# Attention in steps of two units, routing-table products behind their marks

## The chip, the core and the metric

One NeuronCore of a Trainium2 chip runs the whole program. The metric is the device time in microseconds (us) of one execution. The kernel before took 796.1 us, the median of three runs (795.92 to 799.77). Of the core's engines this kernel uses TensorE (PE, with its weight loads PEld), VectorE (DVE), ScalarE (ACT), GpSimd (POOL) and the DMA queues of SyncE (SP) and GpSimd.

## The reference

An attention with a global and a local window, followed by a mixture of experts with the two best of eight.

```
scores = q @ k.T / sqrt(64) - slope[h] * dist          # 4 x 8 heads, 768 positions, head size 64
keep   = (key < n_global) | (0 <= row - key < n_local)  # 8 global, 96 local
a      = softmax(where(keep, scores, -1e9));  x = a @ v  # -> 3072 tokens x 512
noisy  = x @ w_gate + log1p(exp(x @ w_noise)) * noise   # 3072 x 8
top2 weights = softmax over the two largest of noisy
out[token] += weight * relu(x[token] @ w1[e]) @ w2[e]   # for the token's two experts, 512 -> 1024 -> 512
```

## The kernel before, in words

Every engine's instructions run in the order in which the program writes them; semaphores hold an instruction until its inputs are there. Nothing reorders them, so an instruction that waits holds all behind it on its engine.

**Attention.** The 3072 rows are 24 groups of 128, and a group has four units of two heads: 96 units. `score(n)` makes the scores of units n and n+1 on TensorE (L609); VectorE adds the bias and takes the minimum of the negated scores (L616), ScalarE takes exponentials (L620). `trans(n)` transposes a unit's exponentials with four 128x128 products (L632), and ScalarE copies them back (L634). `attend(n)` multiplies them with the values in tiles of 64 columns (L654); after every second unit VectorE divides by the sums (L660 to L663). The loop takes one unit per step: `trans(n)`, at even n `score(n + 2)`, `attend(n - 2)`, then what `todo` lists for this step. `tick()` is called between these and four times inside `score`; each call lets the active routings go one step on (routings 0 and 1 at every second call).

**Gate.** A finished group goes through `gate_t` (transposes, L285), `gate_l` (products with the gate's weights, L293, copied by ScalarE at L296) and `gate_s` (L299), at m, m + 2 and m + 3, where m is the step after the group's last `attend`.

**Routing.** Five runs of groups (`SEG`) are routed one after the other by the generator `route(r)`. It computes noise and the two best experts on VectorE, positions by products with triangles and ones (L375 to L379), and then for each of its 2 x w slots a *mark* (128x128 one-hot, GpSimd, L408) and an *entry* (128x64, VectorE, L409); products of marks and entries (L415) sum up the table of row numbers, which `find` turns into the lists that gathers use. Routing 2 gives the rows of the first four tiles of expert 0. GpSimd also splits the weights of expert 0 into two halves of precision (`split`, L205 and L206), between marks. `scales` takes the largest weight of each piece by VectorE's reductions (L149).

**Experts.** `up(e, c, f)` makes one of eight groups of hidden units (12 products), for c = 0 (512 tokens) and c = 1 (300 tokens); `down` and `down_t` come back to 512. Ahead of each of the eight first groups of expert 0, `steps_of` says how many steps the two unfinished routings, 3 and 4, are taken on: `[10, 60]` and `[0, 25, 4, 14, 1, 100]`. Then the second tiles of expert 0 and the first of expert 1 are gathered by GpSimd's indirect DMAs, four `down` follow, and the gathered tiles are turned by TensorE. At the end of attention the first four tiles are scaled (`ready`, `rest`) and turned (`turn_pe`, L264 to L267) the same way.

Of the kernel before, what the change touches and what calls it, by code (L numbers as in the profile page):

```python
# [35 lines left out]
def tile_local_global_attention_then_moe(  # L36
# [46 lines left out]
    def bank16(tag, bufs):  # L83
        return psum.tile([P, 1024], F16, name=tag, tag=tag, bufs=bufs)
# [174 lines left out]
    def turn_pe(e, t, ps=None):  # L259
        x = xp.pop((e, t))  # L260
        m = height(t)
        ps = (spare_bank(bank16) if ps is None else ps)[:, :2 * KC * m].rearrange("p (k t) -> p k t", k=2 * KC)
        for k in range(2 * KC):
            nc.tensor.transpose(ps[:, k], x[:m, k * P:(k + 1) * P], ident16[:m, :m])  # L264
        y = place(t, m)
        nc.scalar.activation(y[:, :KC], ps[:, :KC], AF.Copy)  # L266
        nc.vector.tensor_copy(y[:, KC:], ps[:, KC:])  # L267
# [36 lines left out]
    def route(r):  # L304
# [99 lines left out]
        for i in range(w):  # L404
            for j in range(2):
                x = gp.tile([P, P], F16, name="mark", bufs=2 * SW)
                y = gp.tile([P, E * (TT + 1)], F16, name="entry", bufs=2 * SW)
                nc.gpsimd.tensor_scalar(x, row, slf[:, 0, i, j:j + 1], None, op0=OP.is_equal)  # L408
                nc.vector.tensor_scalar(y, col, slf[:, 1, i, j:j + 1], val[:, a + i:a + i + 1],  # L409
                                        op0=OP.is_equal, op1=OP.mult)  # L410
                marks.append((x, y))
                yield
        ps = lg[:, (NT * 2 + SW + 1) * E:(NT * 2 + SW + 1 + TT + 1) * E]
        for i, (x, y) in enumerate(marks):
            nc.tensor.matmul(ps, x, y, start=i == 0, stop=i + 1 == len(marks))  # L415
# [24 lines left out]
    with ExitStack() as actx:  # L440
# [182 lines left out]
        def trans(n):  # L623
            g, hp, b, i = geo(n)
            w = 2 * P if i else P
            ps = bank("at", 2)[:, :2 * w]
            p4 = ps.rearrange("p (x c t) -> p x c t", x=2, t=P)
            x = A.pop(n)
            for s in range(2):
                for c in range(w // P):  # L630
                    a = AW - P if c + 1 == w // P else 0
                    nc.tensor.transpose(p4[:, :, c, s * Q:(s + 1) * Q], x[:, s, a:a + P], ident)  # L632
            AT[n] = aw.tile([P, 512], F32, name="at", bufs=4)[:, :2 * w]
            nc.scalar.activation(AT[n], ps, AF.Copy)  # L634
# [3 lines left out]
        def attend(n):  # L638
            g, hp, b, i = geo(n)
            w = 2 * P if i else P  # L640
            x = AT.pop(n)
            if hp % 2 == 0:
                pav[g, hp // 2] = bank("av", 2)[:, :4 * D1].rearrange("p (h d) -> p h d", h=4)
            ps = pav[g, hp // 2]
            blocks = [(vs[g], P, w - P)]
            if i:
                blocks.insert(0, (vp[g], NP + NG, 0))
            for s in range(2):
                h = 2 * hp + s
                c = slice(h * D1, (h + 1) * D1)  # L650
                for t, kk, c0 in blocks:
                    for y in range(2):
                        a = s * w + c0 + y * Q
                        nc.tensor.matmul(ps[y * Q:(y + 1) * Q, h % 4], x[:kk, a:a + Q], t[:kk, c],  # L654
                                         start=kk < P or not i, stop=kk == P, tile_position=(0, y * Q))
            if hp % 2:
                if hp == 1:
                    XR[g] = gp.tile([P, H, D], F32, name="xr", bufs=2)
                den = aw.tile([P, 4], F32, name="den", bufs=2)
                nc.vector.tensor_scalar(den, ps[:, :, D], 1e-9, None, op0=OP.add)  # L660
                nc.vector.reciprocal(den, den)
                h0 = 2 * hp - 2
                nc.vector.tensor_mul(XR[g][:, h0:h0 + 4], ps[:, :, :D],  # L663
                                     den[:, :, None].to_broadcast([P, 4, D]))
# [3 lines left out]
        def at(n, f, *a):  # L668
            todo.setdefault(n, []).append((f, a))
# [70 lines left out]
        if not windowed:  # L740
            gate_consts()
            route_consts()
            empty_rows()
            for j in range(NZ):
                zero_out(j)
            for g in range(NT):
                whole(g)
            load_w(5)
            for x in 1, 2:
                for _ in scales(0, x):  # L750
                    pass
            for j in range(FC):
                split(0, 1, j)
            load_w()
            for t in range(TA):
                ready(0, t)
                rest(0, t)
                turn_pe(0, t)
        else:
            NPAIR = NT * HP  # L760
            LAG = 2
            for k in range(HP):
                at(k, biases, bias, dist, (2 * k, 2 * k + 1))
            at(4, gate_consts)
            at(10, route_consts)
            at(12, empty_rows)
            for g in range(NT):
                b, i = divmod(g, NB)
                n = g * HP
                if g + 3 < NT:  # L770
                    at(n + 2, load_v, g + 3)
                m = n + HP - 1 + LAG + 1
                if g + 1 < NT:
                    at(m, gate_t, g)
                    at(m + 2, gate_l, g)
                    at(m + 3, gate_s, g)
                if i % NBH == 0 and g + NBH < NT:
                    for k in range(NBH):
                        at(n + 4 * k, load_qk, *divmod(g // NBH + 1, 2), k)
                for r, (a, z) in enumerate(SEG):  # L780
                    if g == z - 1:
                        routes[m + 3] = route(r)
            for j in range(NZ):
                at(16 + 9 * j, zero_out, j)
            for j in 20, 26, 32, 46, 64, 76:
                at(j, load_w)
            for x, places in (1, (30, 32, 37, 39, 42, 45)), (2, (44, 46, 56, 58, 61, 64)):
                first = scales(0, x)
                for j in places:
                    at(j, next, first)  # L790
            for j in range(FC):
                at(48 + 2 * j, split, 0, 1, j, nc.gpsimd)
            for t in range(TA):
                at(NPAIR - 5 + t, ready, 0, t)
                at(NPAIR - 4 + min(t, 2), rest, 0, t)

            score(0)
            for n in range(NPAIR + LAG):
                if n < NPAIR:
                    trans(n)  # L800
                if n % 2 == 0 and n + 2 < NPAIR:
                    score(n + 2)
                tick()
                if n == NPAIR - 1:
                    for x, _ in [y for y in active if y[1] <= CLOSE]:
                        for _ in x:
                            pass
                if n >= NPAIR - 1:
                    t = n - NPAIR + 1
                    turn_pe(0, t, bank16("sc", 3))  # L810
                    if t == 2:
                        turn_pe(0, 3, bank16("sc", 3))
                if LAG <= n:
                    attend(n - LAG)
                tick()
                for f, a in todo.pop(n, []):
                    f(*a)
                if n in routes:
                    active.append((routes.pop(n), [z for a, z in SEG].index((n - LAG - 4) // HP + 1)))
            assert len(routes) == 1  # L820
            pending = (pending + [x for x, _ in active] + list(routes.values()))[-2:]


    with ExitStack() as mctx:
# [71 lines left out]

        steps_of = [10, 60], [0, 25, 4, 14, 1, 100]

        for f in range(FC):
            for x, n in enumerate(steps_of):
                if f < len(n):
                    for _ in range(n[f]):
                        next(pending[x], 0)
            if NZ + f < (DUMP + N) // P // 2:
                zero_out(NZ + f)
            if f == 0:
                load_w()
            if f == 2:  # L910
                for h in range(2):
                    nc.scalar.activation(xpb[32:, h * Dm:(h + 1) * Dm], zero[32:MP], AF.Copy)
            up(0, 0, f, f < 3, {4: gate_t, 8: gate_l, 11: gate_s} if f == 0 and windowed else {})
            for j in range([0, 0, 0, 2, 3, 4, 6, 7][f], [0, 0, 2, 3, 4, 6, 7, 8][f]):
                split(0, 2, j)
        for t in range(TB):
            gather(0, TA + t)
        for t in range(2):
# [163 lines left out]
```

## Time and profile before

| | |
|---|---|
| median of the runs shown | 796.1 us |
| profiled execution | 794.64 us, its span 792.8 us |
| TensorE busy | 741.3 us, 93% of the span |
| VectorE, ScalarE, GpSimd busy | 487.8, 360.1, 212.5 us |
| mean granted TensorE clock | 0.981 |
| attention ends, expert 0 begins | 211.67 us |
| expert 0's first eight groups end | 251.86 us |

A busy time is the union of an engine's instruction times. The granted clock is the share of full speed that TensorE got. Waits are given with the engine that waited, the line it stood at and what released it.

### The profile page before, as it was taken

Reading aid. Unit: us, or ns where it says so; the run is one execution under the profiler, and the core shown is the slowest. Engines: PE = TensorE matmul, PEld = TensorE weight load, DVE = VectorE, ACT = ScalarE, POOL = GpSimd, SP = SyncE. Lnnn points to the kernel's source line nnn. Section 1 sums busy time; section 2 is a strip of 40 time slices with the busy share of each in tenths; the row PEclk is TensorE's granted clock in tenths of the full one; section 3 lists DMA queues with packets and bytes.
Section 4 is the critical chain, followed back from the end, with each engine's and each line's share of the span. In section 5 each row is a group of like instructions: output and inputs, shape, how many; then the busy total and the mean of one; then the engine's idle time right before and its main releaser. Section 6 shows DMA issues by size and latency. Waiting matters only on the chain.

```text
span 792.8 us, 16589 instructions
## 1 busy us (share of the span) xinstructions
PE 741.3 (93%) x6279; PEld 460.0 (58%) x6279; DVE 487.8 (62%) x1635; ACT 360.1 (45%) x744; POOL 212.5 (27%) x225
## 2 busy tenths in 40 slices
PE   6999969888849988999999999999999999999995
PEld 4777747666514465556465564656556465565662
DVE  6557877867665466676386476738737664872500
ACT  5777767666432343433345244333424434342411
POOL 2000085241233412221403213141331314122013
PEclk9999989999988999999999999999999999999999
DMA  7899766762602596468448755745964684472015
GB/s 214 283 284 303 207 202 200 227 208 67 222 20 58 87 214 135 135 131 176 99 133 144 124 173 100 165 99 147 142 130 155 104 162 97 109 101 32 1 16 74
DMA packets 107257, 112.58 MB, mean 142 GB/s; under 512 B 53184, under 2 KB 65680, under 8 KB 107168
## 3 DMA queue, kind: packets, MB, share of 16 engines
q1 hardware_dynamic: 95232, 84.51, 39.1%
q0 software_dynamic: 11936, 26.92, 19.5%
q8 instruction: 51, 0.84, 0.4%
q14 instruction: 38, 0.31, 0.1%
HBM read 71.61 MB, written 28.10 MB: 126 GB/s over the span
## 4 chain that ended last, share of the span: by engine, by line
PE 48%; issue 10%; POOL 2%; DVE 1%; DMA 0%; ACT 0%; POOLq 0%; ACTq 0%
PE av L873 14%; PE sc L840 12%; PE at L840 12%; PE av L883 8%; POOL out_dram L858 2%; PE lg L894 0%; PE sc L894 0%; DMA out_dram<-y,ids 0%; DVE wmx L149 0%; PE sc L160 0%; ACT w1h L203 0%; DVE xp L249 0%; PE sc L153 0%; DVE l L238 0%; POOL xg L222 0%
## 5 line engine op out<-in xcount | busy, mean ns | idle before, releaser
L858 POOL DMA_INDIRECT out_dram<-y,ids x56 | 88.7, 1584 | 238.4 <-ACT y L857 234.8
L840 PEld LDWEIGHTS <-w1h 128*128 128x128 f16 x1024 | 100.1, 99 | 70.2 <-issue 4.0
L840 PE MATMUL at<-xx,w1h 128*128 128x300 f16 (+1 forms) x512 | 129.7, 342 | 0.9 <-ACT xx L266 0.8
L840 PE MATMUL sc<-xx,w1h 128*128 128x300 f16 (+1 forms) x512 | 126.2, 335 | 0.0
L222 POOL DMA_INDIRECT xg<-xd,ids x56 | 58.1, 1038 | 169.9 <-DVE hl L851 103.7
L873 PE MATMUL av<-w2h,hh 128*128 128x512 f16 x256 | 97.1, 379 | 0.0
L873 PE MATMUL av<-w2l,hh 128*128 128x512 f16 x256 | 97.0, 379 | 0.0
L873 PE MATMUL av<-w2h,hl 128*128 128x512 f16 x256 | 97.0, 379 | 0.0
L840 PE MATMUL at<-xx,w1l 128*128 128x512 f16 (+1 forms) x256 | 87.1, 340 | 0.0
L620 ACT ACTIVATE a<-ns,mx 128x168 f32<-128x168 f32 (+1 forms) x192 | 70.1, 421 | 35.7 <-DVE mx L616 28.0
L840 PE MATMUL sc<-xx,w1l 128*128 128x512 f16 (+1 forms) x256 | 85.8, 335 | 0.0
L873 PEld LDWEIGHTS <-hh 128*128 128x128 f16 x512 | 49.5, 98 | 56.3
L851 DVE SCALAR_TENSOR_TENSOR hl<-sc,hh 128x300 f16<-128x300 f32 (+1 forms) x63 | 36.4, 577 | 69.3 <-ACT hh L850 69.3
L850 ACT ACTIVATE hh<-at 128x300 f16<-128x300 f32 (+1 forms) x62 | 31.1, 502 | 100.4 <-PE at L840 100.4
L149 DVE TENSOR_REDUCE wmx<-raw 128x1 f32<-128x1024 f32 x64 | 76.4, 1207 | 0.0
L883 PE MATMUL av<-hl,w2h 128*128 128x300 f16 x256 | 74.1, 290 | 2.0 <-DVE hl L851 2.0
L883 PE MATMUL av<-hh,w2h 128*128 128x300 f16 x256 | 74.6, 291 | 0.6 <-DVE yt L886 0.3
L883 PE MATMUL av<-hh,w2l 128*128 128x300 f16 x256 | 74.3, 290 | 0.0
L840 PEld LDWEIGHTS <-w1l 128*128 128x128 f16 x512 | 50.6, 99 | 39.0 <-issue 2.4
L851 DVE SCALAR_TENSOR_TENSOR hl<-at,hh 128x300 f16<-128x300 f32 (+1 forms) x62 | 35.6, 574 | 60.9 <-ACT hh L850 60.9
L616 DVE CUSTOM_DVE_ANT_0 ns<-sc,bias 128x168 f32<-128x168 f32 (+1 forms) x192 | 54.3, 319 | 23.0 <-PE sc L609 18.0
L242 ACT ACTIVATE xp<-xg,up 128x512 f16<-128x512 f32 x48 | 34.5, 719 | 74.1 <-DVE up L240 61.4
(173 smaller groups left out, 1234.6 us busy)
## 6 DMA issues: line engine op xcount, KB each, us to landing
raw<-in_w SPq DMA_DIRECT2D x32, 1024.0 KB
out_dram<-zero SPq DMA_DIRECT2D x14, 512.0 KB
vs<-in_v SPq DMA_DIRECT2D x24, 260.0 KB
qs<-in_q SPq DMA_DIRECT2D x24, 256.0 KB
xd<-xr SPq DMA_DIRECT2D x24, 256.0 KB
ks<-in_k SPq DMA_DIRECT2D x20, 272.0 KB
vp<-in_v SPq DMA_DIRECT2D x20, 195.0 KB
ks<-in_k SPq DMA_DIRECT2D x4, 464.0 KB
```

Of the source, the lines that this page charges most:

```text
L149: nc.vector.tensor_reduce(m[:, i:i + 1], t[:, i % 2 * n:(i % 2 + 1) * n], op=OP.max, axis=AX.X, apply_absolute_value=True)
L222: nc.gpsimd.indirect_dma_start(out=xg[e, t], out_offset=None, in_=xd[:n], in_offset=bass.IndirectOffsetOnAxis(ap=rows(e, t), axis=0), boun ...
L242: nc.scalar.activation(y[:m, :Dm], x[:, :Dm], AF.Copy, scale=u)
L616: nc.vector.tensor_tensor_reduce(out=ns[:, s, :w], in0=ps[:, s], in1=bias[:, hp, s] if i else bias0[:, hp, s], scale=-scale, scalar=3e38, ...
L620: nc.scalar.activation(A[m][:, s, c:c + w], ns[:, s, :w], AF.Exp, bias=mx[:, s:s + 1], scale=-1.0)
L840: nc.tensor.matmul(ps, w[e % 2][:, k, fs], xx[c][:, x + k, :hh[c].shape[2]], start=n == 0, stop=n == 3 * KC - 1)
L850: nc.scalar.activation(hh[c][:, f], ps, AF.Relu)
L851: nc.vector.scalar_tensor_tensor(hl[c][:, f], ps, 0.0, hh[c][:, f], op0=OP.max, op1=OP.subtract)
L858: ins = nc.gpsimd.indirect_dma_start(out=out, out_offset=bass.IndirectOffsetOnAxis(ap=rows(e, t), axis=0), in_=y, in_offset=None, bounds_c ...
L873: nc.tensor.matmul(ps, x[0][:, f, cols], w[e % 2][:, f], start=n == 0, stop=n == 3 * FC - 1)
L883: nc.tensor.matmul(ps, w[e % 2][:, f, cols], x[1][:, f], start=n == 0, stop=n == 3 * FC - 1)
```

## The change

The attention loop takes two units per step: both `trans`, then `score`, then both `attend`, then the todo lists of both. The products of a table come 8 steps of the routing (2 for the later ones) behind its last mark, and every second mark is made by VectorE. `gate_s` moves to m + 4, the routing's start with it. Weight loads, scales, splits and zero fills get other steps. Routing 4's products of positions and its marks move to the sixth group of expert 0, its table behind the eighth.

```diff
-                nc.gpsimd.tensor_scalar(x, row, slf[:, 0, i, j:j + 1], None, op0=OP.is_equal)
+                (nc.vector if j else nc.gpsimd).tensor_scalar(x, row, slf[:, 0, i, j:j + 1], None, op0=OP.is_equal)
...
+        for _ in range(8 if r < CLOSE else 2 if r + 1 < len(SEG) else 0):
+            yield
         ps = lg[:, (NT * 2 + SW + 1) * E:(NT * 2 + SW + 1 + TT + 1) * E]
...
-                    at(m + 3, gate_s, g)
+                    at(min(m + 4, NPAIR + LAG - 1), gate_s, g)
...
-                        routes[m + 3] = route(r)
+                        routes[m + 4] = route(r)
             for j in range(NZ):
-                at(16 + 9 * j, zero_out, j)
-            for j in 20, 26, 32, 46, 64, 76:
+                at(56 + 4 * j, zero_out, j)
+            for j in 22, 32, 50, 58, 76, 86:
                 at(j, load_w)
-            for x, places in (1, (30, 32, 37, 39, 42, 45)), (2, (44, 46, 56, 58, 61, 64)):
+            for x, places in (1, (34, 36, 42, 44, 46, 48)), (2, (58, 60, 66, 68, 70, 72)):
...
-                at(48 + 2 * j, split, 0, 1, j, nc.gpsimd)
+                at(52 + 2 * j, split, 0, 1, j, nc.gpsimd)
...
-            for n in range(NPAIR + LAG):
+            for n in range(0, NPAIR + LAG, 2):
                 if n < NPAIR:
                     trans(n)
-                if n % 2 == 0 and n + 2 < NPAIR:
+                    trans(n + 1)
+                if n + 2 < NPAIR:
                     score(n + 2)
                 tick()
...
+                for u in range(2):
+                    if n == NPAIR:
+                        turn_pe(0, u, bank16("sc", 3))
+                    if n >= LAG:
+                        attend(n - LAG + u)
+                    tick()
+                if n == NPAIR:
+                    for t in range(2, TA):
+                        turn_pe(0, t, bank16("sc", 3))
+                for u in range(2):
+                    for f, a in todo.pop(n + u, []):
+                        f(*a)
                 tick()
...
-        steps_of = [10, 60], [0, 25, 4, 14, 1, 100]
+        steps_of = [10, 60], [0, 25, 0, 0, 0, 18]
...
+        for _ in pending[1]:
+            pass
         for t in range(TB):
             gather(0, TA + t)
```

## Rows read from the trace of the kernel before

**Rows 1.** The page: span and instructions.
```profile
span 792.8 us, 16589 instructions
```

**Rows 2.** Windows: stretch, length, busy PE, PEld, DVE, ACT, POOL (instructions), clock, DMA share, GB/s.
```profile
98.70:121.92 23.22, 16.48 (x231) 12.06 (x230) 15.64 (x76) 13.86 (x34) 19.68 (x22) 0.85 0.56 177
121.92:152.73 30.81, 29.41 (x522) 22.80 (x521) 26.50 (x159) 24.22 (x61) 16.10 (x18) 1.00 0.76 237
152.73:193.58 40.85, 36.19 (x571) 27.20 (x571) 28.18 (x191) 26.53 (x65) 10.94 (x15) 0.96 0.51 161
193.58:211.67 18.09, 13.00 (x204) 10.63 (x204) 16.17 (x72) 9.91 (x21) 5.49 (x9) 0.91 0.34 112
211.67:251.86 40.19, 28.07 (x133) 12.15 (x134) 19.38 (x78) 12.58 (x23) 12.97 (x15) 0.83 0.23 79
17.53:63.63 46.10, 45.54 (x777) 34.90 (x777) 26.09 (x158) 35.75 (x94) 1.73 (x8) 1.00 0.90 278
63.63:98.70 35.07, 33.54 (x596) 25.98 (x595) 29.68 (x167) 25.47 (x66) 1.09 (x1) 1.00 0.78 244
```

**Rows 3.** Waits of all engines: engine, line, releaser, total us, times, longest.
```profile
...
PE lg L299 <- ACT ls L296: 7.1, 8, 1.6
...
```

**Rows 4.** Timeline of PE: start us, length us, engine, line, instruction.
```profile
...
39.65 0.80 PE L609 MATMUL sc<-ks,qs 64*64 64x168 f32 x16
40.38 0.34 PE L654 MATMUL av<-vp,at 104*64 104x65 f32 x4
40.55 0.29 PE L654 MATMUL av<-vs,at 128*64 128x65 f32 x4
40.66 0.29 PE L654 MATMUL av<-vp,at 104*64 104x65 f32 x4
...
41.00 0.66 PE L285 MATMUL sc<-ident,xr 128*128 128x128 f32 x4
41.49 0.60 PE L632 MATMUL at<-ident,a 128*128 128x128 f32 x4
42.02 0.34 PE L654 MATMUL av<-vp,at 104*64 104x65 f32 x4
...
42.63 0.65 PE L632 MATMUL at<-ident,a 128*128 128x128 f32 x4
43.22 0.80 PE L609 MATMUL sc<-ks,qs 64*64 64x168 f32 x16
...
```

**Rows 5.** Timeline: the exponentials of that pair, and of a later one.
```profile
...
40.97 1.41 ACT L620 ACTIVATE a<-ns,mx 128x168 f32<-128x168 f32 x4 [0.56 <-DVE mx L616]
...
63.63 0.80 PE L609 MATMUL sc<-ks,qs 64*64 64x168 f32 x16
...
65.68 1.41 ACT L620 ACTIVATE a<-ns,mx 128x168 f32<-128x168 f32 x4 [1.00 <-DVE mx L616]
...
```

**Rows 6.** Timeline around the first routing table's products.
```profile
...
110.20 1.16 POOL L206 TENSOR_TENSOR w1l<-raw,w1h 128x512 f16<-128x512 f32 x1
...
110.35 1.04 DVE L409 TENSOR_SCALAR entry<-col,slf,val 128x64 f16<-128x64 f16 x1
...
110.70 0.38 PE L415 MATMUL lg<-entry,mark 128*128 128x64 f16 x7
...
117.20 0.24 PE L415 MATMUL lg<-entry,mark 128*128 128x64 f16 x1 [3.17 <-POOL mark L408]
...
```

**Rows 7.** Timeline in expert 0's first half, and a group from the chain.
```profile
...
223.22 0.19 PE L375 MATMUL lg<-ohs,upper 128*128 128x8 bf16 x2 [5.17 <-DVE ohs L358]
...
231.66 0.18 DVE L382 TENSOR_TENSOR po<-lg,carry 128x32 f32<-128x32 f32 x1
...
233.84 1.75 DVE L409 TENSOR_SCALAR entry<-col,slf,val 128x64 f16<-128x64 f16 x8
233.91 5.14 POOL L408 TENSOR_SCALAR mark<-row,slf 128x128 f16<-128x128 f16 x8 [3.38 <-DVE slf L401]
...
311.87 2.59 PE at L840 x12
...
```

More of the change, by code (lines that the diff above doesn't have):

```diff
@@ L797, in tile_local_global_attention_then_moe @@
             score(0)
-            for n in range(NPAIR + LAG):
+            for n in range(0, NPAIR + LAG, 2):
                 if n < NPAIR:
                     trans(n)
-                if n % 2 == 0 and n + 2 < NPAIR:
+                    trans(n + 1)
+                if n + 2 < NPAIR:
                     score(n + 2)
                 tick()
-                if n == NPAIR - 1:
+                if n == NPAIR:
                     for x, _ in [y for y in active if y[1] <= CLOSE]:
@@ L807, in tile_local_global_attention_then_moe @@
                             pass
[L808 to L814, printed above, removed]
+                for u in range(2):
[4 more added lines that the diff above has]
+                    tick()
+                if n == NPAIR:
+                    for t in range(2, TA):
[3 more added lines that the diff above has]
+                        f(*a)
                 tick()
[L816 to L819, printed above, removed]
+                for u in range(2):
+                    if n + u in routes:
+                        active.append((routes.pop(n + u), [z for a, z in SEG].index((n + u - LAG - 5) // HP + 1)))
             assert len(routes) == 1
```

## The prediction

> **What bounds the kernel now.** First the span of the page [rows 1], then busy time by stretches, in seven windows cut at the starts of score blocks [rows 2]. From 17.53 to 63.63 us (13 pairs of units) TensorE is busy 45.54 of 46.10 us at a granted clock of 1.00, with VectorE at 26.09 and ScalarE at 35.75: TensorE is the bound, at 46.10 / 13 = 3.55 us a pair. From 63.63 to 98.70 (9 pairs) a pair takes 3.90. From 98.70 to 193.58 (21 pairs, 23.22 + 30.81 + 40.85 = 94.88 us) it takes 4.52, TensorE is idle for 12.8 us, and the clock drops to 0.85 and 0.96 in the stretches with the gaps. The end of attention, 18.09 us, and the first half of expert 0, 40.19 us, have TensorE busy for 13.00 and 28.07 us, at 0.91 and 0.83. So the time before 252 us holds some 30 us of idle TensorE and a halved clock after it; from there on TensorE runs nearly without gaps and the change touches nothing.
>
> The waits and the timeline of the widest gap tell who holds it up: gate_s stands for its ScalarE copy, 7.1 us in 8 waits [rows 3], and the routing tables' products stand for GpSimd's marks [rows 6]. Then the order inside a pair [rows 4] and its chain [rows 5], read from timelines.
>
> **Merging two units.** A pair now runs transposes T, scores S, products A, T, A; then it runs T, T, S, A, A. Two changes of kind vanish, one after an A and one after a T. Their price is in the starts [rows 4]. gate_t's four 128x128 transposes followed by others of that shape take 41.49 - 41.00 = 0.49 us; the same four followed by an A take 42.02 - 41.49 = 0.53. A's quarters follow each other by 0.11 to 0.17 us (40.38, 40.55, 40.66), so four take some 0.47 and A takes 41.00 - 40.38 = 0.62 when something else follows: 0.15. Ahead of an S they take 43.22 - 42.63 = 0.59. So a T that is followed by its own kind saves 0.04 to 0.10, an A some 0.15. Together that is 0.19 to 0.25; A's part rests on the quarters' mean, good to 0.05, so 0.14 and 0.30 are the bounds and I take 0.22.
>
> A new limit appears. The second unit's T now stands ahead of the next S. In a quiet pair S starts at 39.65 and its fourth exponential ends at 40.97 + 1.41 = 42.38, 2.73 us later [rows 4, 5]; then two transposes (half of 0.49) and the change to S, some 0.1: 3.1 us between two S. TensorE's own work, 3.55 - 0.22 = 3.33, is longer, so quiet pairs gain the 0.22. Before, S waited only for the first unit's exponentials. With a weight reduction in VectorE's way the fourth one ends at 65.68 + 1.41 = 67.09, 3.46 after S at 63.63 [rows 5]: such a pair can't be shorter than 3.46 + 0.37 = 3.83.
> (a) 17.53 to 63.63: 13 x 0.22 = **2.9 us** (0 to 3.9).
> (b) 63.63 to 98.70: 9 x 0.22 = 2.0, and gate_s waits of some 1.8, a quarter of the 7.1 of [rows 3], that go (gate_s two units behind gate_l has a whole pair over its copy; in the pair's own todo it would follow gate_l at once): **3.8** (0 to 6).
>
> **Tables behind their marks.** The first table's products start at 110.70 and the last at 117.20, for 12 products [rows 6]: 6.5 us, of which seven in a run show that they need no more than 0.1 each. The marks stood behind weight splits in GpSimd's queue; 8 more steps at every second tick are two pairs, some 7 us, and the mark comes from two engines. Six marks instead of twelve leave GpSimd 3.6 us less to do (5.14 / 8 = 0.64 each [rows 7]). So the wait goes, 6.0. If the splits still stand in front it stays: 763.5 + 6 = 769.
> What TensorE could gain in the 94.88 us: 6.0; of the clock that [rows 2] show missing, 23.22 x 0.15 + 40.85 x 0.04 = 5.1, the half that lay in busy time, 2.5; gate_s 3.6 (half of 7.1); 21 x 0.22 = 4.6: together 16.7. But VectorE has 15.64 + 26.50 + 28.18 = 70.3 us of work there [rows 2], and gets 20 marks. A mark on VectorE is not in the trace: an entry, half as wide, costs 1.75 / 8 = 0.22 [rows 7], so it is 0.22 to 0.44, near the entry: 0.25, 5 us in all. Two weight reductions (1.2 us each) that stood earlier now fall in this stretch: 77.7. VectorE in order cannot be busy all the time between S and the exponentials; its densest stretch now is 26.50 of 30.81, 86% [rows 2], and I allow 90%: 77.7 / 0.9 = 86.4.
> (c) 98.70 to 193.58: 94.88 - 86.4 = **8.5** (2 to 16.7). Late here are VectorE's routing operations, not TensorE.
> Moved DMAs: five zero fills (0.5 MB) and one weight load (1 MB) leave the stretch before 63.63, where DMA is busy 0.90 [rows 2], for stretches at 0.51 to 0.76; scores' inputs are asked 8 units ahead, which hides them, and costs 1 to 2 us if it doesn't.
>
> **End of attention.** Route 3's table product leaves it for the place behind expert 0's first group, and gate_s no longer holds TensorE; VectorE (16.17 of 18.09 us busy [rows 2]) gives up route 3's last steps, 3.9 us by the same steps of route 4 (from 231.66 to 233.84 + 1.75 [rows 7]), but keeps the gathered tokens' scaling, which the turns wait for. (d) **2.8** (0.5 to 4.5).
>
> **Expert 0's first half.** A full group is 2.59 us [rows 7]; eight are 20.7, and the gate inside the first adds 1.0. The 40.19 us also hold the positions' product waiting 5.17 for VectorE's one-hot and the last table waiting for marks that end at 233.91 + 5.14 = 239.05 [rows 7], and two groups behind these waits at a half clock. After the change the positions' product stands four groups (10.4 us) behind the chain that made it wait 5.17 + 2.59, so it waits no more. The table product stands three groups, 7.8 us, behind the positions. VectorE's chain from the positions to the last entry took 233.84 + 1.75 - 231.66 = 3.9 [rows 7], plus four marks, 5; but VectorE starts it behind earlier residuals and weight splits, which ScalarE feeds late since its own queue waits for routing, so I leave 1.4 us of wait (0 to 4). Route 3's table before group 1 waits 0.9 and costs 0.6; positions 0.4; the last table 0.6. Sum: 20.7 + 1.0 + 0.4 + 0.6 + 1.4 + 0.6 + 0.9 = 25.6. (e) 40.19 - 25.6 = **14.6** (10 to 15.6).
> What is late next: the row numbers come behind the last group instead of ahead of it, and behind the table on TensorE stand the down products, which take the wait of 1.4 in full. The gathers for expert 0's second part are needed only after four down products, 20 us; and residuals of groups 5 to 7 stand behind the marks on VectorE, but down reads them 3 us into its first product. I charge nothing; without that cover it is 2 to 3 us, in (e)'s lower end.
>
> **Sum.** 2.9 + 3.8 + 8.5 + 2.8 + 14.6 = 32.6 us. The profiled execution took 794.64 (span 792.8 [rows 1] and 1.84 around it), which gives 762.0; the median of the runs shown, 796.1, is 1.5 above it, so **763.5 us**.
>
> **A rule of the Trainium skill against this change.** In the trace an entry on VectorE begins at 110.35, takes 1.04 us instead of 0.22, and ends at 111.39, just behind GpSimd's two-input subtraction, 110.20 + 1.16 = 111.36; but eight entries beside GpSimd's own marks take their usual 0.22 [rows 6, 7]. The Trainium skill (SBUF — State Buffer, Who interferes with whom) says that a VectorE operation in a two-port mode and a GpSimd operation exclude each other, the second one standing still for the other's whole length. By it every mark on VectorE would wait for one on GpSimd. The trace bears it out for the subtraction alone, which can stop only one VectorE operation each time, as it does now.
>
> **Rivals.**
> VectorE keeps up: attention is bound by TensorE alone, (c) brings 16.7: 763.5 - 8.2 = 755. For it: 86% is no proven limit. Against: 77.7 us of work in a stretch of 77.
> Merging gains nothing: the chain of exponentials, with routing between its four steps, takes back what the order saves; (a) and (b) 0, (c) 3.0, (d) 0.5, (e) 14.6: 18.1, 796.1 - 18.1 = 778. For it: the pair of [rows 5] with 3.83. Against: 13 quiet pairs at 3.1.
> Marks lock VectorE out: each of 24 marks waits 0.64 us for one on GpSimd, 15 us that land on a full VectorE or on the table: 763.5 + 15 = 778. Against: the eight entries.
> The table still waits for marks behind the splits: 769.
> Slower: the second unit's T, ahead of the next S, makes each pair wait for VectorE's routing. It decides where a pair under routing exceeds my lengths, 4.1 us, by 1.1 (32.6 us over 30 pairs); at 1.3 it is 39 us, 802. For it: the last exponential can come 0.73 late [rows 5]. Against: that is with a 1.2 us reduction ahead, and the other operations are 0.2 us.
>
> **Chances.** Forecast 0.58 (752 to 774); VectorE keeps up 0.15; merging gains nothing 0.13; table still waits 0.05; marks lock 0.05; slower 0.04. The range 750 to 779 leaves out the best end of (c) and (e) together and the slower case. A change of 0.5% (4 us) can be told from none: faster 0.95, same 0.01, slower 0.04.
>
> **What would show it.** In the changed profile: no idle time before the first table's products and before gate_s; the last routing's positions and table products with waits under 2 us each; expert 0's eight groups within 26 us at a granted clock near 1; quiet pairs at 3.3 us; pairs under routing near 4.1 with VectorE near 90% busy. Wrong would be quiet pairs still at 3.55, marks over 0.4 us on VectorE, or new waits of the second part of expert 0 for gathered rows.

## The result, and the profile after

The changed kernel took 764.3 us, the median of four runs (761.75 to 768.78), against 796.65: a ratio of 0.959 (95% interval 0.954 to 0.9645), faster by 32.4 us. The prediction was 763.5. The profiled execution, 768.78 us, was the longest of the four, while that of before (794.64) was 2.0 below its median: the two profiles show 25.9 us of the 32.4. The page's span:

```profile
span 767.1 us, 16631 instructions
```

Windows of the changed kernel at the same blocks of scores as [rows 2], with the same columns:

```profile
94.20:109.26 15.06, 14.16 (x222) 9.95 (x221) 13.92 (x79) 12.53 (x32) 8.40 (x9) 1.00 0.86 268
109.26:140.98 31.72, 29.49 (x533) 22.69 (x532) 29.05 (x154) 25.39 (x65) 20.96 (x20) 1.00 0.82 254
140.98:183.23 42.25, 36.72 (x575) 27.86 (x575) 30.91 (x206) 27.07 (x65) 8.06 (x10) 0.92 0.65 217
183.23:200.51 17.28, 12.60 (x191) 10.05 (x191) 14.74 (x76) 9.31 (x20) 0.81 (x1) 0.80 0.38 123
200.51:226.68 26.17, 25.00 (x141) 11.80 (x142) 18.95 (x89) 13.44 (x25) 9.22 (x12) 0.94 0.29 103
19.29:61.38 42.09, 42.06 (x778) 34.16 (x777) 24.30 (x155) 35.20 (x92) 1.73 (x8) 1.00 0.84 267
61.38:94.20 32.82, 30.89 (x591) 25.16 (x590) 26.20 (x156) 24.76 (x66) 1.09 (x1) 1.00 0.68 209
```

Stage by stage in the order of the prediction: (a) 46.10 to 42.09 us, (b) 35.07 to 32.82, (c) 94.88 to 89.03, (d) 18.09 to 17.28, (e) 40.19 to 26.17. Ahead of (a) pair 4 (counted from 0) starts 1.76 us later than before, and behind (e) 0.6 is gained.

The PE timeline of a quiet pair of the changed kernel, to hold against [rows 4]:

```profile
22.57 0.80 PE L611 MATMUL sc<-ks,qs 64*64 64x168 f32 x16
23.30 0.34 PE L656 MATMUL av<-vp,at 104*64 104x65 f32 x4
...
24.38 0.43 PE L293 MATMUL sc<-xt,wgn 128*32 128x128 f32 x8
24.74 1.09 PE L634 MATMUL at<-ident,a 128*128 128x128 f32 x8
```

Two A in a row take 24.38 - 23.30 = 1.08 us where two single ones took 2 x 0.62, and two T up to the next S (22.57 + 3.19 = 25.76) take 1.02 where they took 0.59 + 0.53 or more. Quiet pairs alternate 3.19 (with gate_l) and 3.50 (with gate_s and gate_t).

The PE timeline where [rows 6, 7] had their waits:

```profile
117.90 0.52 PE L417 MATMUL lg<-entry,mark 128*128 128x64 f16 x12
...
216.34 0.20 PE L375 MATMUL lg<-ohs,upper 128*128 128x8 bf16 x2
...
224.69 0.23 PE L417 MATMUL lg<-entry,mark 128*128 128x64 f16 x2
...
226.49 0.35 PE L417 MATMUL lg<-entry,mark 128*128 128x64 f16 x2 [0.34 <-DVE mark L408]
```

All twelve products of the first table run in 0.5 us, the last routing's positions wait for nothing, and its table costs some 2 us behind the eighth group.

### The profile page after: what moved, and what is told of

Its sections match the earlier page's. It is cut to its first block, busy times and chain, and to the rows that moved or that the text cites. A ratio compares the mean times of both kernels' runs of the same rounds, so it can differ in the third digit from the quotient of the medians.

```text
span 767.1 us, 16631 instructions
## 1 busy us (share of the span) xinstructions
PE 731.9 (95%) x6279; PEld 457.2 (60%) x6279; DVE 488.5 (64%) x1659; ACT 359.7 (47%) x744; POOL 197.5 (26%) x201
## 4 chain that ended last, share of the span: by engine, by line
PE 47%; issue 11%; DVE 3%; POOL 2%; DMA 0%; ACT 0%; POOLq 0%
PE av L880 14%; PE sc L847 12%; PE at L847 12%; PE av L890 8%; POOL out_dram L865 2%; DVE wmx L149 1%; DVE w2l L208 1%; PE lg L901 1%; PE sc L901 0%; DMA out_dram<-y,ids 0%; PE sc L160 0%; DVE hl L858 0%; ACT w1h L203 0%; DVE l L238 0%; DVE xp L249 0%
## 5 line engine op out<-in xcount | busy, mean ns | idle before, releaser
L847 PE MATMUL at<-xx,w1h 128*128 128x300 f16 (+1 forms) x512 | 127.6, 337 | 0.9 <-ACT xx L266 0.8
```

The source lines that it names most:

```text
L847: nc.tensor.matmul(ps, w[e % 2][:, k, fs], xx[c][:, x + k, :hh[c].shape[2]], start=n == 0, stop=n == 3 * KC - 1)
```

## The experiments

Stages named p4, p17, p26, p47 begin at the scores of these pairs, as the windows above do. Each result gives the median in us and its ratio to the kernel before, with the 95% interval in brackets.

**The loop alone.** The kernel before with this of the change and nothing else:

```diff
-                    at(m + 3, gate_s, g)
+                    at(min(m + 4, NPAIR + LAG - 1), gate_s, g)
-            for n in range(NPAIR + LAG):
+            for n in range(0, NPAIR + LAG, 2):
...
```

> The kernel before with the loop in steps of two units and gate_s and the routing's start at m + 4, all else as before (marks on GpSimd, tables right behind them, old places of loads and fills, expert 0 as before). Theory, that two changes of kind in a pair cost TensorE 0.22 us or more and gate_s's waits go: quiet pairs at 3.3 us instead of 3.55, 8 to 12 us in all, so 785 to 789; the first table's wait of 6 us stays. Rival, that the chain of exponentials takes it back: 794 or more, with pairs under routing longer than 4.5 us.

783.6 us, ratio 0.985 (0.9815 to 0.989), 11 us faster, a little better than expected. Quiet pairs gain the whole of what the full change gains, and the first table's wait stays (windows p4 to p17 and p26 to p47, then PE's timeline):

```profile
18.71:60.89 42.18, 42.14 (x777) 34.23 (x776) 25.09 (x156) 35.19 (x92) 1.73 (x8) 1.00 0.94 302
...
93.92:183.45 89.53, 79.30 (x1327) 62.15 (x1326) 67.25 (x417) 64.86 (x160) 46.75 (x54) 0.94 0.63 201
```

```profile
116.25 0.23 PE L415 MATMUL lg<-entry,mark 128*128 128x64 f16 x1 [3.17 <-POOL mark L408]
```

**Expert 0's part alone.** The kernel before with `steps_of = [10, 60], [0, 25, 0, 0, 0, 18]` and the rest of routing 4 behind the eighth group.

> The kernel before with the new places of routing 4's steps alone. Theory: both waits of expert 0's first half and the slow clock behind them go and the gathers stay hidden behind four down products: 40.2 us become about 27, so 783. Rival, that the later row numbers hold the gathers and what needs them: idle TensorE behind the fourth down product, 787 or more.

784.6 us, 0.987 (0.983 to 0.990): 10.2 us, less than the 13 expected. Its two windows, the eight groups and what follows up to the second half:

```profile
212.12:240.02 27.90, 23.80 (x134) 11.09 (x134) 19.18 (x74) 13.40 (x25) 10.20 (x12) 0.97 0.29 104
240.02:265.81 25.79, 25.03 (x125) 11.52 (x125) 13.57 (x39) 6.81 (x11) 14.43 (x12) 0.90 0.52 107
```

The first gains 12.3. The second is 2.4 longer than before (23.37), with TensorE busy and the granted clock at 0.90 instead of 1.00. Here all eight marks come from GpSimd, and the wait for the table is longer than in the changed kernel: from 234 to 240 us TensorE is busy for 1.90 us, and from 240 to 245, where the down products begin, the granted clock is 0.51, half speed. No wait for gathered rows appears, so the rival falls.

**No lag, all marks on GpSimd**, else as changed:

```diff
-        for _ in range(8 if r < CLOSE else 2 if r + 1 < len(SEG) else 0):
-            yield
-                (nc.vector if j else nc.gpsimd).tensor_scalar(x, row, ...)
+                nc.gpsimd.tensor_scalar(x, row, ...)
```

> The changed kernel with all marks on GpSimd and the tables' products right behind the last mark. Theory: the first table waits 6 us again and the clock falls behind it, less the 5 us that VectorE gets back from the marks it no longer makes: 766 to 772. Rival, VectorE's load decides and the wait is hidden in pairs that wait anyway: 760 to 764.

772.6 us, 0.973 (0.969 to 0.977), 8 above the changed kernel. The pair with the first table takes 11.67 us instead of 3.9, but later pairs are shorter than the changed kernel's, so of that only 2.1 stays in the stretch from p26 to p47 (some 5.7 if a stop of TensorE of some 3.6 us in the changed kernel, see the end, is taken off); 4.6 more are lost in expert 0. The windows of the two:

```profile
91.00:182.10 91.10, 80.21 (x1327) 61.92 (x1326) 69.27 (x420) 64.50 (x160) 46.91 (x54) 0.94 0.73 233
199.09:229.90 30.81, 26.77 (x143) 12.18 (x143) 21.25 (x89) 13.78 (x25) 14.84 (x20) 0.89 0.25 91
```

**Old places** of loads, fills, reductions and splits in the changed kernel (20, 26, 32, 46, 64, 76 for the loads, and so on, as the minus lines of the diff).

> The changed kernel with weight loads, zero fills, reductions of weights and splits at their old steps. Theory: these moves carry nothing, 764 within 3 us. Rival, that DMA traffic before 63 us (busy share 0.90) or two more reductions ahead of unit 36 hold pairs that are now shorter: 768 or more, lost before 100 us. Second rival: the later places cost VectorE two reductions in its full stretch, so the old ones gain 2 us or more.

761.4 us, 0.958 (0.955 to 0.960). This is 2.9 below the changed kernel, as much as the second rival said, but the two intervals overlap. By stages, p17 to p26 takes 31.82 us instead of the 30.5 that the new places have without a stop of TensorE, and p26 to p47 takes as long as in the changed kernel once its stop of some 3.6 us (see the end) is taken off 89.03:

```profile
92.32:177.90 85.58, 77.57 (x1327) 59.21 (x1326) 72.48 (x433) 65.06 (x160) 37.35 (x38) 0.98 0.66 210
```

So the moves bring some 1.3 us in the one stage, and in all nothing that these runs can show.

**gate_s right behind gate_l**: `at(m + 3, gate_s, g)`.

> The changed kernel with gate_s at m + 3, which in steps of two units is right behind gate_l. Theory: TensorE then waits in every group for ScalarE's copy, which stands behind four exponentials, and both transposes stand behind gate_s: 0.5 to 0.9 us a group over 23 groups, 774 to 785. Rival: the pair waits for its exponentials anyway, so gate_s hides in that wait: 764 to 768.

778.3 us, 0.978 (0.972 to 0.984). Quiet pairs alternate 3.27 and 4.19 us instead of 3.50 and 3.19; in PE's timeline:

```profile
40.33 0.40 PE L299 MATMUL lg<-sel,ls 128*128 128x16 f32 x2 [0.70 <-ACT ls L296]
```

Merging without moving gate_s would have given back 14 us.

**All marks on GpSimd, with the lag**: only the mark's line as in the diff of two experiments above.

> The changed kernel with the lag of the tables kept and all marks on GpSimd. Theory, VectorE is the limit under routing: attention from 94 us gets 3 to 5 us shorter, and expert 0's first half 3 to 5 us longer, since routing 4's eight marks come one by one: 764 within 2 us. Rival, VectorE has room there: attention stays, and only expert 0 loses: 767 to 769. Second rival: with the marks back in GpSimd's queue behind the splits the lag is too short, and the first table waits again: 770.

767.2 us, 0.964 (0.959 to 0.968). Both halves came as the theory said: p26 to p47 4.5 us shorter than in the changed kernel (some 1.3 of it a shorter stop of TensorE, see the end), expert 0 4.5 longer. The total lies just above the theory's 762 to 766. The first table does not wait again. The windows of the two:

```profile
92.18:176.70 84.52, 77.40 (x1327) 58.75 (x1326) 70.10 (x420) 64.64 (x160) 46.83 (x54) 1.00 0.77 251
192.95:223.61 30.66, 25.98 (x142) 11.89 (x142) 21.77 (x92) 13.77 (x25) 14.85 (x20) 0.94 0.27 95
```

**More load on VectorE**, under routing and where none runs. In `tick()`, with the bounds 50 to 92 and 6 to 32:

```diff
+            if 50 <= pair[0] < 92:
+                nc.vector.tensor_copy(spin[:, 32:], spin[:, :32])
```

> The changed kernel with one more small VectorE copy (128x32) at every tick of units 50 to 91, 168 copies of 0.1 to 0.2 us, which compute nothing. Theory, VectorE and the chain through it set the pairs under routing: 10 to 25 us longer, nearly what the copies take. Rival, TensorE's order sets them: under 4 us.

> The changed kernel with the same copies at every tick of units 6 to 31, 104 of them, where no routing runs. Theory: quiet pairs alternate between 3.50 (TensorE's own work) and 3.19 (near the chain of exponentials, 3.1); three copies ahead of the fourth exponential lift the chain to 3.4 to 3.6, so the short pairs grow and the long ones hardly: 2 to 4 us in all. Rival, VectorE's load sets these pairs: 10 us or more. Second rival, TensorE alone does: 0.

Under routing: 778.6 us, 0.976 (0.971 to 0.982), 14 us; without: 765.6, 0.960 (0.954 to 0.965), 1.3 us. The stretch from p26 to p47 of the one, from p4 to p17 of the other:

```profile
91.62:197.38 105.76, 88.30 (x1326) 64.33 (x1325) 91.87 (x600) 67.65 (x160) 37.41 (x38) 0.92 0.63 201
```

```profile
18.44:62.31 43.87, 43.31 (x777) 34.00 (x777) 36.34 (x258) 36.05 (x92) 1.73 (x8) 1.00 0.81 253
```

168 copies add 91.87 - 73.88 = 18.0 us to VectorE, and 16.7 of them appear in the stretch (73.88 and 89.03 are the sums of the changed kernel's three windows). In quiet pairs 104 copies add 12.0 us, and 1.8 appear. VectorE sets the pairs under routing; TensorE and the chain set the quiet ones. The quiet stretch's 1.8 us is a little under the 2 to 4 expected, and the 1.3 of the medians is within the noise: with copies between them the four exponentials, ScalarE's work, take 1.51 us instead of 1.41 (first with the copies, then the changed kernel), and the fourth ends 2.83 us after its S (at 24.96) instead of 2.73 (at 22.57), so the chain did not grow to 3.4. Two short pairs take 4.26 and 3.63 us, the others grow by 0.1 or less.

```profile
26.28 1.51 ACT L626 ACTIVATE a<-ns,mx 128x168 f32<-128x168 f32 x4 [0.56 <-DVE mx L622]
```

```profile
23.89 1.41 ACT L622 ACTIVATE a<-ns,mx 128x168 f32<-128x168 f32 x4 [0.41 <-DVE mx L618]
```

**Marks split by routing**: `(nc.vector if j and r > CLOSE else nc.gpsimd)`, VectorE helps where TensorE waits for the table, in routings 3 and 4.

> The changed kernel with every second mark on VectorE for routings 3 and 4 alone; routings 0 to 2 mark on GpSimd, with the lag. Theory: attention as short as with all marks on GpSimd (84.5 us from 94 us on instead of 88.8) and expert 0 as short as in the changed kernel (26.2 instead of 30.7): 759 to 761. Rival, the gains are of one execution: 763 to 765.

758.8 us, 0.9525 (0.948 to 0.957), the fastest version: its median is 5.5 us below the changed kernel's, each against its own runs of before, though the two intervals overlap. p26 to p47 is 3.3 us shorter than with the old places (85.58), where no stop of TensorE falls into it either. Windows of that stretch and of expert 0's first groups:

```profile
91.47:173.75 82.28, 76.43 (x1326) 58.40 (x1325) 69.99 (x420) 64.58 (x160) 46.85 (x54) 1.00 0.81 258
...
190.71:217.90 27.19, 25.98 (x141) 11.92 (x142) 19.07 (x91) 13.45 (x25) 9.26 (x12) 0.89 0.29 103
```

**Routing steps behind the exponentials**, on top of it: score's four `tick()` calls after its loop.

> As the marks split by routing, and the four ticks inside score behind its four exponentials instead of between them: the same VectorE work, in another order. Theory, the chain S, minimum, exponential, transposes sets pairs under routing: its fourth exponential falls from 3.2 to 3.7 us back to 2.8, and 21 pairs gain 0.2 to 0.4 us: 4 to 8 us less, 752 to 757. Rival, VectorE's load as such sets them: no gain, 759 to 762.

763.5 us, 0.957 (0.953 to 0.961): 4.7 slower than the split marks, so the theory falls. The stretch from p26 to p47 takes 85.32 us, 3.0 more. The routing's products on TensorE are issued in these same ticks, and wait longer for steps that stand further back on VectorE (the split marks, then this run). These waits are 1.3 us of the 3.0; the rest is not traced, and what the chain alone costs under routing stays open, since the move shifts both.

```profile
146.85 0.19 PE L375 MATMUL lg<-ohs,upper 128*128 128x8 bf16 x2 [0.51 <-DVE ohs L358]
...
151.50 0.45 PE L417 MATMUL lg<-entry,mark 128*128 128x64 f16 x10 [0.99 <-DVE carry L383]
```

```profile
147.98 0.19 PE L375 MATMUL lg<-ohs,upper 128*128 128x8 bf16 x2 [1.33 <-DVE ohs L358]
...
154.75 0.45 PE L417 MATMUL lg<-entry,mark 128*128 128x64 f16 x10 [1.50 <-DVE carry L383]
```

**Scaling two units earlier**, on top of the split marks: `at(NPAIR - 7 + t, ready, 0, t)`, `at(NPAIR - 6 + min(t, 2), rest, 0, t)`.

> As the marks split by routing, and the first four tiles' scaling (ready, rest) two units earlier. Theory, at attention's end TensorE waits for ScalarE's copies that stand behind this scaling (3.2 us in the changed kernel): the last 17 us get 2 to 4 shorter: 756 to 758. Rival, the gathered rows are not there yet or VectorE's last routing needs that time: no gain or 1 to 2 us lost: 759 to 762.

760.4 us, 0.953 (0.949 to 0.957): no gain. The wait moves from the copies of the last units to their exponentials, which now stand behind the scaling on ScalarE:

```profile
181.51 1.97 PE L634 MATMUL at<-ident,a 128*128 128x128 f32 x8 [3.50 <-ACT a L622]
```

**Both on top.**

> Marks split by routing, ticks behind the exponentials and the scaling two units earlier, all together. Theory: the gains add, 749 to 755. Rival, they share a cause and the sum is that of the better one: 755 to 758.

763.5 us, 0.958 (0.954 to 0.962): the loss of the one, and nothing from the other.

## Why the prediction was right, point by point

**(a), 2.9, measured 4.0.** Right, undersized: a quiet pair saves 3.55 - 42.09 / 13 = 0.31, just above the upper bound of 0.30. The starts above give 0.16 for the two A and 0.10 for the two T; the other 0.05 is not traced. The loop alone gives nearly the same stretch, 42.18. The chain's limit of 3.1 matters little here: T now waits for exponentials, 15.1 us in the whole execution against 2.5 before, but 9.0 of them fall between p26 and p47 and 1.3 into this stretch.

```profile
PEld at L634 <- ACT a L622: 15.1, 36, 1.3
```

**(b), 3.8, measured 2.25** in the profiled execution, which holds one stop of TensorE of 1.93 us (below); kernels with the same loop and the new places, and without that stop, take 30.5 us, a gain of 4.6. The waits of gate_s for its copy are gone but for one, 0.5 us in the whole execution instead of 7.1 [rows 3]:

```profile
PE lg L299 <- ACT ls L296: 0.5, 1, 0.5
```

**(c), 8.5, measured 5.85.** That VectorE is the bound is shown: 16.7 of 18.0 us of added VectorE load appear, and with this stretch's marks taken off VectorE it is some 3.3 us shorter. The terms were off in opposite directions. VectorE's work was 73.9 us, not 77.7, and sixteen marks fall into the stretch, not twenty; but VectorE is busy for 83% of it, not 90%. In part that is a stop of TensorE: pair 44 takes 7.06 us, and 3.49 with the split marks. Without these 3.6 us the stretch would be some 85.5 us by estimate, with VectorE 86% busy, the densest share of before.

How the gain divides was not foreseen. Of the kernels without a stop of TensorE here, the one with only expert 0's part changed takes 94.80 us, the loop alone 89.53 with its table still waiting. The lag is worth more than its 6.0: with the marks on GpSimd it takes the stretch from 91.10 (no lag) to 82.28 (split marks). The marks on VectorE give some 3.3 of that back, and in the profiled execution the stop some 3.6.

Most marks on VectorE take 0.24 to 0.28 us, near the 0.25 assumed. But six of the 24 take over 0.4, which the prediction named as a sign of being wrong, and the sixteen of this stretch take 5.65 us, 0.35 each. Two take 0.65, both beside GpSimd's two-input subtraction; one of them:

```profile
104.06 0.65 DVE L408 TENSOR_SCALAR mark<-row,slf 128x128 f16<-128x128 f16 x1
```

```profile
103.49 1.16 POOL L206 TENSOR_TENSOR w1l<-raw,w1h 128x512 f16<-128x512 f32 x1
```

It ends at 104.71, just behind the subtraction's 104.65. Beside GpSimd's own marks a mark mostly keeps its length (twice it took 0.42 and 0.46), so the rival in which each mark waits for one on GpSimd fell.

**(d), 2.8, measured 0.8.** Route 3's table left the stretch, and the longest wait of gate_s in it fell from 1.62 to 0.46 us (before, then after):

```profile
198.62 0.40 PE L299 MATMUL lg<-sel,ls 128*128 128x16 f32 x2 [1.62 <-ACT ls L296]
```

```profile
200.07 0.61 PE L299 MATMUL lg<-sel,ls 128*128 128x16 f32 x2 [0.46 <-ACT ls L296]
```

But ScalarE's copies of the last units now stand behind the scaling, which waits for VectorE (PE, then ACT):

```profile
194.03 0.48 PE L656 MATMUL av<-vp,at 104*64 104x65 f32 x4 [3.24 <-ACT at L636]
```

```profile
192.77 0.72 ACT L242 ACTIVATE xp<-xg,up 128x512 f16<-128x512 f32 x1 [1.85 <-DVE up L240]
```

That wait was not in the prediction, which let only the turns wait for the scaling; it is the step of (d) that failed. The lower clock behind it reaches into (e), whose first group takes 205.98 - 200.51 = 5.47 us with route 3's table, instead of 3.62 without it before.

**(e), 14.6, measured 14.0.** Right, including the table's 2 us behind the eighth group (the sum had 1.4 of wait and 0.6 of work) and the gathers that stay hidden: what follows takes 23.36 us, as before (23.37). Of it 4.5 us, about a third, need the marks from two engines, as the kernel with all marks on GpSimd shows.

The five terms sum to 32.6 as predicted and to 26.9 in the profiled execution, less 1.76 at the start and plus 0.6 at the end. The medians' 32.4 lie closer to the forecast than the profile's terms do, since that execution was 4.5 us above its median. Its two stops of TensorE, 1.93 and some 3.6 us, would cover that, but no profile of an execution at the median shows it. That the forecast lies within 1 us of the median is in part luck: the start's 1.76 us had no term, and (d) brought 2.0 too little, while (a) brought 1.1 too much. Where the start's 1.76 us come from was not tried; the other kernels with the new loop start pair 4 at 18.4 to 19.5 us, those with the old one at 17.5 and 18.0.

## What to carry to other kernels

Price a regrouping on TensorE from the starts in the trace, then write down the chain that the new order closes; here the first gave the gain and the second, with VectorE's queue in it, set how much of it was kept. Give an engine's spare time to another only in the stretch where it is spare: the same kind of marks cost 3 us under routing and save 4.5 in expert 0. When two steps are put into one, look which product then stands right behind the copy that it needs: gate_s alone was worth 14 us.

## What the hardware showed that was not expected

TensorE stops in the middle of a run of equal products, with no semaphore to wait for (PE's timeline of the changed kernel):

```profile
69.88 0.41 PE L293 MATMUL sc<-xt,wgn 128*32 128x128 f32 x5
72.23 0.41 PE L293 MATMUL sc<-xt,wgn 128*32 128x128 f32 x3 [1.93 <-issue]
```

VectorE goes on meanwhile. A longer one, between 170 and 174 us, has TensorE stop five times for 0.24 to 0.42 us; from 173.1 to 176.5 the granted clock is 0.50, and that pair is 7.06 us long. The kernel before has its like near 178 (a pair of 6.35), and so have three of the other profiles (pairs of 5.47 to 6.55); eight others have pairs of 3.5 to 3.8 there. GpSimd gathers the rows of routing 2 in these microseconds, but it does so in the split marks' profile too, which has no stop. What the engine waits for in these stops no run shows.
